# Block attention feeding a gated MLP: a place of its own for the odd tile's probabilities, and attention work in other slots

## Chip, cores, metric

One core of one Trainium2 chip runs the kernel. The metric is the device time of one execution in microseconds (us), the median over several runs; the kernel before took 499.02 us (three runs, 496.99 to 500.42). The engines are named as in the profile: PE (TensorE matmul), PEld (its weight loads), DVE (VectorE), ACT (ScalarE), POOL (GpSimd), SP (SyncE, whose queue issues all DMAs here).

## The reference

`q`, `k`, `v` are (8 batches, 8 heads, 576 positions, 64). Attention is local: each block of 64 positions attends to itself alone. Its output, heads side by side, is `x` (8, 576, 512), the input of a gated MLP:

```python
scores = scale * np.matmul(q_c, k_c.transpose(0, 1, 2, 4, 3))      # blocks of 64 positions
attn = np.exp(scores - np.max(scores, axis=-1, keepdims=True))
attn = attn / (np.sum(attn, axis=-1, keepdims=True) + 1e-09)
x = np.matmul(attn, v_c)                                           # -> (B, S, 512)
h = gelu(x @ w_in)                                                 # 512 -> 1024
u, v = h[..., :512], h[..., 512:]
v_n = (v - mean(v)) / np.sqrt(var(v) + 1e-06) * g_ln
v_s = np.einsum('ts,bsd->btd', w_sg, v_n) + b_sg[None, :, None]
out = x + (u * v_s) @ w_out
```

## The kernel before

**Tiles.** The 8 x 576 positions are 36 tiles of 128 positions, two blocks of 64 each. Two batches hold 9 tiles: 0 to 3 belong to the even batch, tile 4 is half of each, 5 to 8 belong to the odd batch. Tiles 0 and 1, 2 and 3, 5 and 6, 7 and 8 go as pairs; tile 4 goes by itself (the single tile). Further on, tile 9 is tile 0 of the next two batches, tile 13 is their single tile.

**Attention of a tile** has three steps, in code and tables named by a letter and the tile. S (`att_scores`): 16 matmuls of 64x64 for each tile into PSUM, then the softmax: maximum, subtraction, sums and reciprocal on DVE, exponential on ACT, normalization on DVE or POOL. T (`att_transpose`): DVE transposes 32x32 blocks, ACT and DVE copy them into the buffer `ptT`. O (`att_out`): 16 matmuls of 64x64 for each tile with the values `av`, after which `keep` writes `xh` (rounded) and `xf` on ACT and `xl` (the remainder) on DVE. Tiles 0 to 4 of the first two batches go through `first_scores` and a transpose on PE; tile 2 of these has its softmax on ACT, 16 small instructions.

**Buffers.** Probabilities `pt` have one buffer (tag "pt", bufs=1) for pairs and single tiles alike, so a single tile's softmax starts to write when the pair ahead has been read by its T, and the pair behind waits for the single tile. `ptT` has one buffer too, with two places. `av` has two buffers, one for each tile: the loads of a tile's values wait until O of the tile two ahead has read.

**MLP of a batch.** Units follow each other: v (5 or 4 units of 12 matmuls with 512 columns), u0 to u4, s0 to s3 and o0 to o2 (groups of 12 or 28 matmuls with 288 columns; u and o use products of sums of blocks, `tx`, `ts`, `wx`). `ORDER` fixes them. The list `SLOTS` says after which unit of a batch a step S, T or O of the tiles ahead is recorded: for odd batches key 1, for even ones key 0. The first two batches and the loading of the weights (W, w: v half of w_in; X, x: u half; Y: w_out) follow the list `START`. `REST_V` says for each quarter of the v half whether the low part is made by PE alone (p) or by DVE (v); with p, PE does one f32 matmul with `ident` more.

**What sets the order.** Nothing is issued as recorded. `Plan` collects every instruction, gives each a cost and a due time, and `run` fills the engines' queues; the result is a fixed order for each engine, DMAs included (all on SP's queue). `EARLY` shifts due times of named steps by thousands of ns. PE may take work from up to 10 us further down its list. Every instruction therefore carries one line number, L250, in the profile, and tiles' names tell them apart: `pm` is any PSUM tile, `qk` the queries and keys.

Of the kernel before, what the change touches and what calls it, by code (L numbers as in the profile page):

```python
# [12 lines left out]
F32 = mybir.dt.float32  # L13
# [11 lines left out]
B, H, S, D = 8, 8, 576, 64  # L25
P = 128
# [18 lines left out]


START = """
A0 L0 B0 A1 L1 L2 L3 B1 A2 A3 S0 W0 T0 S1 W1 S2 w0 w1 T1 W2 O0 O1 W3 w2 T2 S3 M0 w3 v00 O2 A4 T3 X0 O3 G0 S4 v01 A8 T4
O4 B8 x0 X1 v02 X2 x1 v03 X3 U1 v04 U0 x2 g0 g1 x3 g2 g3 P5 g4 F0 u02 u03 s00 T5 F1 T6 P7 s01 s02 Q5 T7 T8 s03 Q7 v10
v11 Y0 v12 v13 Y4 Y2 Y1 Y3 u10 u11 s10 u13 Y5 s11 Y6 Y7 u12 A10 s12 P9 B10 A12 o01 s13 T9 T10 o02 P11 A14 V0 V1 V2 V3  # L50
o03 o00 Q9 B12 T11 o10 o11 T12 B14 S13 A15 o12 Q11 o13 T13
"""

SUMS = {7: 0, 10: 1, 11: 2, 12: 3}
X_SUMS = {0: 0, 2: 1, 4: 2}

PE_TILES = 5

# [5 lines left out]

SLOTS = {1: "0:T0 3:S23 6:T2 8:T1 10:O01 12:S4 12:T3 14:O23 14:T4", 0: "0:O4 2:S56 5:T5 8:T6 9:S78 9:T7 10:O56 11:S9A 14:T8 14:O78"}


ON_POOL = ("a", "c", "n1", "n2", "n4", "t",)  # L70
# [10 lines left out]
G_BLOCK = {(0, 0): 0, (1, 0): 1, (1, 1): 2, (0, 1): 3}  # L81


REST_V, REST_U = "vppp", "pgvg"
ENGINES = ("tensor", "vector", "scalar", "gpsimd", "sync")
EARLY = {'X*': -8, 's03': 1, 'Y0': -2, 'P7': 3, 'v04': -4, 'X0': -1, 'w3': -1, 'W*': -1, 'g4': 5, 'Y7': -2}
AHEAD = 10000
SWITCH = 150
HORIZON = 25000
LATE, DMA_LATE = 60, 3000  # L90
WAIT = {"tensor": 100 + LATE, "gpsimd": 120 + LATE}
TABLES = {AF.Exp: 1, AF.Gelu_apprx_tanh: 2}
# [305 lines left out]
def block_attention_gated_mlp(ctx: ExitStack, tc: tile.TileContext, qkv, w_in, w_out, w_sg, g_ln, b_sg, out):  # L398
# [6 lines left out]
    att = pool("att", 2)  # L405
# [291 lines left out]
                nc.sync.dma_start(out=vts[t][j * D : (j + 1) * D, c * HP : (c + 1) * HP], in_=src)  # L697

    scale = 1.0 / math.sqrt(D)
    first_pts = att.tile([P, 3, H, D], F32, name="first_pts", tag="pt", bufs=1)  # L700
    first_ptT = att.tile([P, 2, HP, P], F32, name="first_ptT", tag="ptT", bufs=1)

    def att_scores(*tiles):

        if tiles[0] < PE_TILES:
            for t in tiles:
                first_scores(t)
            return
# [12 lines left out]
        nc.vector.tensor_reduce(by_slot, sc, axis=AX.X, op=ALU.max, negate=True)
        pt = att.tile([P, n, H, D], F32, name="pt", tag="pt", bufs=1)
        for i in range(n):
            nc.vector.tensor_tensor(
                pt[:, i].rearrange("p (c hp) s -> p c hp s", c=2), sc[:, :, i],
                by_slot[:, :, i].unsqueeze(3).broadcast_to([P, 2, HP, D]), op=ALU.add,
            )
        nc.scalar.activation(pt, pt, AF.Exp, scale=scale)
        den = nmax.rearrange("p (i h) -> p i h", i=n)
        nc.vector.tensor_reduce(den, pt, axis=AX.X, op=ALU.add)  # L730
        nc.vector.tensor_scalar(den, den, SM_EPS, None, op0=ALU.add)
        nc.vector.reciprocal(den, den)
        for i, t in enumerate(tiles):
            eng = pick("a") if t > last[1] else nc.vector
            eng.tensor_tensor(pt[:, i], pt[:, i], den[:, i].unsqueeze(2).broadcast_to([P, H, D]), op=ALU.mult)
            pts[t] = pt[:, i]

    def first_scores(t):

        qt = qks.pop(t)  # L740
        sc = ps_m.tile([P, 2, 512], F32, name="pm")[:, :, : HP * D].rearrange("p c (g s) -> p c g s", g=HP)
        for x in range(2):
            for e in range(2):
                for y in range(2):
                    for c in range(2):
                        h, j = 4 * x + 2 * y + e, (y + c) % 2
                        r, o = slice(c * D, (c + 1) * D), slice(j * D, (j + 1) * D)
                        nc.tensor.matmul(sc[o, c, 2 * x + e, :], qt[r, 0, h, :], qt[r, 1, h, :], start=True, stop=True)
        nd = small.tile([P, 2, H], F32, name="nmax", tag="nmax")
        nmax, den = nd[:, 0], nd[:, 1]  # L750
        by_slot = lambda a: a.rearrange("p (c hp) s -> p c hp s", c=2)
        nc.vector.tensor_reduce(nmax.rearrange("p (c hp) -> p c hp", c=2), sc, axis=AX.X, op=ALU.max, negate=True)
        pt = first_pts[:, t % 3]
        if t in ACT_SOFTMAX:
            nc.vector.tensor_scalar(nmax, nmax, scale, None, op0=ALU.mult)
            for h in range(H):
# [12 lines left out]
        pts[t] = pt

    ptTs = {}

    def att_transpose(t):
        pt = pts[t]
# [437 lines left out]
    for b in range(2, B):  # L1212
# [4 lines left out]
        for i, ((f, k), after) in enumerate(zip(units, slots)):  # L1217
# [61 lines left out]
```

## Time and profile before

| | |
|---|---|
| runs | 496.99, 499.02, 500.42 us; median 499.02 |
| profiled execution | 497.11 us, of which 495.3 us from its first to its last instruction (the span) |
| PE busy | 477.0 us (96%), 5076 matmul records |
| PE weight loads | 436.1 us |
| DVE, ACT, POOL busy | 421.4, 313.9, 127.4 us |
| granted TensorE clock | 0.999 of full speed over the span |
| ACT table loads | 34, 43.6 us |

Matmuls overlap in the records, so the pace of PE is read from the distance between the starts of two matmuls, not from the duration of one. An f32 matmul of the program stands as two records in the trace, the 64x64 ones too (1152 in the program, 2304 records).

### The profile page before, as it was taken

Reading aid. Unit: us, or ns where it says so; the run is one execution under the profiler, and the core shown is the slowest. Engines: PE = TensorE matmul, PEld = TensorE weight load, DVE = VectorE, ACT = ScalarE, POOL = GpSimd, SP = SyncE. Lnnn points to the kernel's source line nnn. Section 1 sums busy time; section 2 is a strip of 40 time slices with the busy share of each in tenths; the row PEclk is TensorE's granted clock in tenths of the full one; section 3 lists DMA queues with packets and bytes.
Section 4 is the critical chain, followed back from the end, with each engine's and each line's share of the span. In section 5 each row is a group of like instructions: output and inputs, shape, how many; then the busy total and the mean of one; then the engine's idle time right before and its main releaser. Section 6 shows DMA issues by size and latency. Waiting matters only on the chain.

```text
span 495.3 us, 12328 instructions
## 1 busy us (share of the span) xinstructions
PE 477.0 (96%) x5076; PEld 436.1 (88%) x5076; DVE 421.4 (85%) x771; ACT 313.9 (63%) x511; POOL 127.4 (26%) x115
## 2 busy tenths in 40 slices
PE   3999999999998999999999999999999999999996
PEld 2567898899997899888999899998999899998996
DVE  7978999997896899999879698988869698878466
ACT  4889598734365688646676587936675577834330
POOL 0104100200470668115301531115301341215000
PEclk9999999999999999999999999999999999999999
DMA  8965103123338504456153815436053823133112
GB/s 327 356 198 164 55 3 73 58 87 96 122 121 269 161 1 123 155 182 192 63 152 105 252 61 216 128 125 185 14 161 108 253 96 130 44 105 119 60 70 95
DMA packets 56140, 65.46 MB, mean 132 GB/s; under 512 B 35602, under 2 KB 45842, under 8 KB 56084
## 3 DMA queue, kind: packets, MB, share of 16 engines
q1 hardware_dynamic: 56084, 64.67, 40.8%
q8 instruction: 40, 0.66, 0.6%
q14 instruction: 16, 0.13, 0.1%
HBM read 52.07 MB, written 12.58 MB: 131 GB/s over the span
## 4 chain that ended last, share of the span: by engine, by line
PE 57%; DVE 26%; ACT 9%; DMA 5%; issue 2%; DVEq 0%; ACTq 0%; SPq 0%
PE pm L250 56%; DVE nmax L250 5%; DMA out_dram<-ot 3%; DVE ot L250 3%; DVE u L250 3%; DVE pt L250 2%; ACT ptT L250 2%; DVE gl L250 2%; DVE sm L250 2%; DVE ts L250 1%; DVE ptT L250 1%; ACT L250 1%; DVE xl L250 1%; DMA av<-qkv 1%; ACT z L250 1%
## 5 line engine op out<-in xcount | busy, mean ns | idle before, releaser
L250 PE MATMUL pm<-wsg,v 128*128 128x288 f32 x768 | 109.4, 297 | 0.0
L250 PEld LDWEIGHTS pm<-wsg,v 128*128 128x128 f32 x768 | 103.8, 188 | 0.9
L250 POOL TENSOR_TENSOR pt<-pt,nmax 128x512 f32<-128x512 f32 x27 | 31.0, 1164 | 162.9 <-DVE nmax L250 145.1
L250 PE MATMUL pm<-gh,wout 128*128 128x288 f32 x272 | 54.5, 299 | 0.8 <-DVE pt L250 0.8
L250 ACT ACT_TABLE_LOAD x34 | 43.6, 1283 | 18.4 <-DVE pt L250 9.3
L250 DVE TENSOR_TENSOR u<-pm,u 128x576 f32<-128x576 f32 x50 | 37.0, 750 | 19.2 <-PE pm L250 18.7
L250 PE MATMUL pm<-win_h,xl 128*128 128x512 f32 x128 | 51.8, 405 | 1.0 <-DVE xl L250 1.0
L250 ACT COPY ptT<-blocks 32x256 f32<-32x256 f32 (+1 forms) x93 | 44.2, 475 | 10.9 <-DVE blocks L250 9.1
L250 PE MATMUL pm<-win_l,xh 128*128 128x512 f32 x128 | 50.8, 397 | 0.0
L250 PE MATMUL pm<-win_h,xh 128*128 128x512 f32 x128 | 50.6, 395 | 0.0
L250 POOL TENSOR_TENSOR sm<-sm,neg_half 128x1 f32<-128x1 f32 x36 | 31.6, 878 | 69.5 <-DVE sm L250 41.5
L250 PEld LDWEIGHTS pm<-gh,wout 128*128 128x128 f32 x272 | 42.5, 188 | 1.8 <-DVE pt L250 1.1
L250 ACT CAST gh<-u 128x576 fp32r<-128x576 f32 x32 | 21.2, 672 | 27.2 <-DVE u L250 25.7
L250 DVE BATCH_NORM_STATS2 sm<-hs 128x6 f32<-128x512 f32 x36 | 24.8, 688 | 12.8 <-ACT hs L250 12.7
L250 PE MATMUL pm<-gl,wout 128*128 128x288 f32 x136 | 34.9, 295 | 0.0
L250 ACT ACTIVATE hs<-pm 128x512 f32<-128x512 f32 x36 | 21.3, 597 | 20.2 <-PE pm L250 13.2
L250 ACT ACTIVATE v<-hs,sm 128x512 fp32r<-128x512 f32 x32 | 23.1, 725 | 16.4 <-POOL sm L250 9.9
L250 PEld LDWEIGHTS pm<-win_h,xl 128*128 128x128 f32 x128 | 24.0, 188 | 7.8 <-DVE xl L250 2.3
L250 DVE TENSOR_TENSOR gl<-u,gh 128x576 fp32r<-128x576 f32 x32 | 25.2, 794 | 6.2 <-ACT gh L250 5.9
L250 PEld LDWEIGHTS pm<-win_h,xh 128*128 128x128 f32 x128 | 24.0, 188 | 5.7
L250 PE MATMUL pm<-xh,win_l 128*128 128x288 f32 x112 | 28.4, 300 | 0.0
L250 PEld LDWEIGHTS pm<-win_l,xh 128*128 128x128 f32 x128 | 24.1, 188 | 4.9
(151 smaller groups left out, 1155.7 us busy)
## 6 DMA issues: line engine op xcount, KB each, us to landing
qk<-qkv SPq DMA_DIRECT2D x31, 512.0 KB, 5.0
out_dram<-ot SPq DMA_DIRECT2D x31, 288.0 KB, 4.6
wx<-kept_u SPq DMA_DIRECT2D x10, 768.0 KB, 8.0
wx<-kept_o SPq DMA_DIRECT2D x10, 768.0 KB, 4.3
av<-qkv SPq DMA_DIRECT2D x116, 64.0 KB, 3.1
wsg<-w_in SPq DMA_DIRECT2D x4, 512.0 KB, 6.7
wout<-w_in SPq DMA_DIRECT2D x4, 512.0 KB, 4.8
st<-w_out SPq DMA_DIRECT2D x8, 256.0 KB, 2.8
```

Source lines behind the costliest of these rows:

```text
L250: getattr(getattr(self.nc, op.engine), op.method)(*op.args, **op.kwargs)
```

## The change

Single tiles get a buffer of their own for probabilities (tag "pt1"), and their transposed probabilities are written back into that buffer instead of `ptT`. In the first tiles the third place of `first_pts` becomes a tile of its own (`third_pt`). `START`, `SLOTS`, `SUMS`, `X_SUMS`, `EARLY` and `HORIZON` get other numbers, and the second quarter of the v half makes its low part on DVE (`REST_V`). The list `START` is long; one line stands for it.

```diff
-A0 L0 B0 A1 L1 L2 L3 B1 A2 A3 S0 W0 T0 S1 W1 S2 w0 w1 T1 W2 O0 O1 W3 w2 T2 S3 M0 w3 v00 O2 A4 T3 X0 O3 G0 S4 v01 A8 T4
+A0 L0 L1 L2 A1 B0 B1 A2 L3 A3 S0 W0 W1 T0 S1 S2 w0 w1 T1 W2 O0 O1 W3 w2 T2 S3 M0 w3 v00 O2 A4 T3 X0 O3 G0 S4 v01 A8 T4
...
-SUMS = {7: 0, 10: 1, 11: 2, 12: 3}
-X_SUMS = {0: 0, 2: 1, 4: 2}
+SUMS = {7: 0, 10: 1, 12: 2, 13: 3}
+X_SUMS = {0: 0, 1: 1, 5: 2}
...
-SLOTS = {1: "0:T0 3:S23 6:T2 8:T1 10:O01 12:S4 12:T3 14:O23 14:T4", 0: "0:O4 2:S56 5:T5 8:T6 9:S78 9:T7 10:O56 11:S9A 14:T8 14:O78"}
+SLOTS = {1: "2:T0 3:T1 6:S23 10:S4 10:O01 12:T2 13:T3 13:O23 14:T4 15:S56 15:O4", 0: "5:T5 8:T6 11:S78 11:O56 12:T7 14:T8 14:S9A 15:O78"}
...
-REST_V, REST_U = "vppp", "pgvg"
+REST_V, REST_U = "vvpp", "pgvg"
...
-EARLY = {'X*': -8, 's03': 1, 'Y0': -2, 'P7': 3, 'v04': -4, 'X0': -1, 'w3': -1, 'W*': -1, 'g4': 5, 'Y7': -2}
+EARLY = {'s03': 1, 'P7': 3, 'v04': -4, 'X0': -1, 'w3': -1, 'g4': 5, 'Y7': -2, 'x0': 8, 'W*': 12, 'X*': 3, 'Y0': -1}
...
-HORIZON = 25000
+HORIZON = 20000
...
-    first_pts = att.tile([P, 3, H, D], F32, name="first_pts", tag="pt", bufs=1)
+    first_pts = att.tile([P, 2, H, D], F32, name="first_pts", tag="pt", bufs=1)
+    third_pt = att.tile([P, 1, H, D], F32, name="third_pt", tag="pt1", bufs=1)
...
-        pt = att.tile([P, n, H, D], F32, name="pt", tag="pt", bufs=1)
+        pt = att.tile([P, n, H, D], F32, name="pt", tag="pt" if n == 2 else "pt1", bufs=1)
...
-        pt = first_pts[:, t % 3]
+        pt = first_pts[:, t % 3] if t % 3 < 2 else third_pt[:, 0]
...
-        if place == 0:
+        if place == 0 and t % 9 != 4:
             ptTs[0] = att.tile([P, 2, H, 2, D // 2], F32, name="ptT", tag="ptT", bufs=1)
...
-        ptT = ptTs[0][:, place]
+        ptT = pt.rearrange("p h (a s) -> p h a s", a=2) if t % 9 == 4 else ptTs[0][:, place]
```

Over the whole program PE has one matmul less (the f32 one with `ident` of the second quarter), DVE one instruction more (that quarter's low part), ACT 30 table loads instead of 34. The 1152 matmuls of 64x64 stand in 48 uninterrupted runs on PE before and in 37 after; up to the end of `START` there are 18 runs in both, behind it 30 before and 19 after.

On PE in batch 4, at the last u product (u4) and the s units around it (`tx`: sums of x; `wsg`, `v`: the s unit's operands; `qk` rows are S of tiles 25 and 26, `ptT` rows O of tiles 23 and 24), this stands before the change:

```order
L250 MATMUL pm_460<-tx_0_436,wx_0_439 128x288
L250 MATMUL pm_469<-qk_450 64x64 x16
L250 MATMUL pm_469<-qk_451 64x64 x16
L250 MATMUL pm_476<-wsg_0_160,v_431 128x288 x2
...
L250 MATMUL pm_476<-wsg_0_160,z1_0_86 128x288 x2
L250 MATMUL pm_477<-ptT_462,av_425 64x64 x16
L250 MATMUL pm_477<-ptT_462,av_435 64x64 x16
L250 MATMUL pm_460<-tx_0_436,win_l_83 128x288
```

The same place on PE after the change:

```order
L250 MATMUL pm_459<-tx_0_440,win_h_82 128x288
L250 MATMUL pm_473<-qk_430 64x64 x16
L250 MATMUL pm_473<-qk_431 64x64 x16
L250 MATMUL pm_478<-ptT_461,av_423 64x64 x16
L250 MATMUL pm_478<-ptT_461,av_434 64x64 x16
L250 MATMUL pm_481<-wsg_0_161,v_438 128x288 x2
```

An s unit stood between S and O; now O follows S without a wide matmul between them.

On PE at the end of `START`, around O of tile 13 (`pm_287` before, `pm_281` after, its values in `av`), where batch 2 begins with its first v unit (`pm_283` before, `pm_291` after), this stands before the change:

```order
L250 MATMUL pm_279<-gh_211,wout_0_194 128x288 x2
L250 MATMUL pm_283<-win_h_82,xl_258 128x512
...
L250 MATMUL pm_283<-win_h_82,xh_257 128x512
L250 MATMUL pm_287<-ptT_281,av_270 64x64 x16
L250 MATMUL pm_293<-win_h_82,xl_258 128x512
```

The same place on PE after the change (`pm_286` is S of tiles 14 and 15):

```order
L250 MATMUL pm_284<-gh_213,wout_0_191 128x288 x2
L250 MATMUL pm_286<-qk_242 64x64 x16
L250 MATMUL pm_291<-win_h_82,xl_259 128x512
...
L250 MATMUL pm_281<-pt_275,av_269 64x64
L250 MATMUL pm_286<-qk_276 64x64 x10
L250 MATMUL pm_281<-pt_275,av_269 64x64 x7
L250 MATMUL pm_286<-qk_276 64x64 x3
L250 MATMUL pm_281<-pt_275,av_269 64x64 x8
L250 MATMUL pm_286<-qk_276 64x64 x3
L250 MATMUL pm_291<-win_h_82,xh_258 128x512
```

O of tile 13 moved from behind the 12 matmuls of the v unit to behind five of them, and S of tile 14 moved ahead of the unit.

On DVE at the start, in the softmax of tile 1 (`nmax_106` before, `nmax_107` after; `wsg` and `wout` hold raw quarters of w_in there, in order wsg_0, wsg_1, wout_0, wout_1), this stands before the change:

```order
L250 TENSOR_TENSOR win_l_83<-wsg_0_94,win_h_82 128x512
L250 TENSOR_SCALAR wsg_1_97<-wsg_1_97 128x512
L250 TENSOR_REDUCE nmax_106<-pm_105 128x8
...
L250 TENSOR_TENSOR xl_115<-banks_90,xh_114 128x4x128
L250 TENSOR_SCALAR wout_0_98<-wout_0_98 128x512
```

The same place on DVE after the change:

```order
L250 TENSOR_TENSOR win_l_83<-wsg_0_95,win_h_82 128x512
L250 TENSOR_SCALAR wsg_1_96<-wsg_1_96 128x512
L250 TENSOR_REDUCE nmax_107<-pm_106 128x8
...
L250 TENSOR_TENSOR xl_116<-banks_90,xh_115 128x4x128
L250 TENSOR_REDUCE nmax_109<-pm_108 128x8
L250 TENSOR_TENSOR win_l_83<-wsg_1_96,win_h_82 128x512
```

The low part of the second quarter (the last row) is new on DVE, ahead of the work on the third and fourth quarter.

## Rows read from the trace of the kernel before

**Rows 1.** The page: the span, the busy time of each engine with its share of the span, and the chain of work that ended last, by engine.

```profile
span 495.3 us, 12328 instructions
...
PE 477.0 (96%) x5076; PEld 436.1 (88%) x5076; DVE 421.4 (85%) x771; ACT 313.9 (63%) x511; POOL 127.4 (26%) x115
...
PE 57%; DVE 26%; ACT 9%; DMA 5%; issue 2%; DVEq 0%; ACTq 0%; SPq 0%
```

**Rows 2.** Busy time by stretch, with its length, then PE, PEld, DVE, ACT and POOL busy us (number of instructions), granted clock, share of the DMA engines, GB/s.

```profile
128.00:160.00 32.00, 30.60 (x421) 28.70 (x423) 27.78 (x43) 17.35 (x29) 15.86 (x13) 1.00 0.55 175
200.00:220.00 20.00, 18.96 (x179) 17.14 (x178) 19.42 (x32) 12.67 (x19) 0.00 (x0) 1.00 0.43 157
...
372.00:440.00 68.00, 67.79 (x786) 63.29 (x787) 59.80 (x108) 46.80 (x71) 16.65 (x14) 1.00 0.37 114
```

**Rows 3.** The waits of PE over the whole span: who waited for whom, us in total, times, the longest.

```profile
PE pm L250 <- DMA qk<-qkv: 6.9, 2, 4.4
...
PE pm L250 <- DMA av<-qkv: 1.3, 1, 1.3
...
PE pm L250 <- DVE pt L250: 0.8, 1, 0.8
```

**Rows 4.** The timeline of PE around one run of 64 records of 64x64: start us, us, instruction, count. Matmuls of 288 columns are on both sides.

```profile
190.92 0.69 PE L250 MATMUL pm<-wsg,z 128*128 128x288 f32 x4
191.54 1.16 PE L250 MATMUL pm<-ptT,av 64*64 64x64 f32 x64
192.63 0.40 PE L250 MATMUL pm<-tx,win_l 128*128 128x288 f32 x1
192.87 0.43 PE L250 MATMUL pm<-tx,win_h 128*128 128x288 f32 x2
```

**Rows 5.** The timeline of PE around a run of 34 records in which two records of S (`qk`) stand among those of O; the first row is its first five, the last row the wide matmul behind it.

```profile
252.04 0.37 PE L250 MATMUL pm<-ptT,av 64*64 64x64 f32 x5
...
252.76 0.40 PE L250 MATMUL pm<-wsg,v 128*128 128x288 f32 x1
```

**Rows 6.** The timeline of DVE in the first 48 us: the low part of the first quarter of w_in, and `xl` of tile 1.

```profile
11.59 0.69 DVE L250 TENSOR_TENSOR win_l<-wsg,win_h 128x512 fp32r<-128x512 f32 x1
...
23.84 0.69 DVE L250 TENSOR_TENSOR xl<-banks,xh 128x512 fp32r<-128x512 f32 x1
```

**Rows 7.** The timeline of ACT in the first 48 us: the first of 16 softmax instructions of tile 2, and `xh` of tile 1 behind them.

```profile
20.86 0.31 ACT L250 ACTIVATE first_pts<-pm,nmax 128x64 f32<-128x64 f32 x1 [0.89 <-DVE nmax L250]
...
23.19 0.62 ACT L250 CAST xh<-banks 128x512 fp32r<-128x512 f32 x1
```

**Rows 8.** The timeline of PE in the first 45 us, in brackets the idle time ahead and what ended it: S of tile 1, an f32 matmul with `ident` (two records) and the next one, the first matmul of the first v unit.

```profile
8.03 1.13 PE L250 MATMUL pm<-qk 64*64 64x64 f32 x32 [2.53 <-DMA qk<-qkv]
...
19.15 1.02 PE L250 MATMUL pm<-wout,ident 128*128 128x512 f32 x2
20.07 0.38 PE L250 MATMUL pm<-wout,low 128*128 128x512 bf16 x1
...
25.02 0.40 PE L250 MATMUL pm<-win_h,xl 128*128 128x512 f32 x1
```

**Rows 9.** The timeline of PE and ACT around O of tiles 7 and 8, and the writing of their `xh`.

```profile
82.42 0.85 PE L250 MATMUL pm<-ptT,qkv_w 64*64 64x64 f32 x32
...
83.62 1.00 PE L250 MATMUL pm<-ptT,qkv_w 64*64 64x64 f32 x32 [0.35 <-issue]
...
84.85 1.01 ACT L250 CAST xh<-pm 128x1024 fp32r<-128x1024 f32 x1
```

**Rows 10.** The timeline of DVE behind it: `xl` of tiles 7 and 8.

```profile
86.81 1.29 DVE L250 TENSOR_TENSOR xl<-pm,xh 128x512 fp32r<-128x512 f32 x2 [0.25 <-ACT xf L250]
```

**Rows 11.** The timeline of PE at the end of `START`: O of tiles 11 and 12, the o unit behind it, the first and the last matmul of the first v unit of batch 2, O of tile 13.

```profile
150.61 1.18 PE L250 MATMUL pm<-ptT,av 64*64 64x64 f32 x64
151.72 0.53 PE L250 MATMUL pm<-gh,wout 128*128 128x288 f32 x2
...
155.01 0.40 PE L250 MATMUL pm<-win_h,xl 128*128 128x512 f32 x1
...
157.58 0.39 PE L250 MATMUL pm<-win_h,xh 128*128 128x512 f32 x1
159.25 0.95 PE L250 MATMUL pm<-ptT,av 64*64 64x64 f32 x15 [1.28 <-DMA av<-qkv]
```

**Rows 12.** The timeline of SP's queue there: start us, us that the issue took, DMA, count. The eight `av` transfers carry tiles 13 and 14.

```profile
152.09 1.16 SPq L250 DMA_DIRECT2D out_dram<-ot  x1
153.34 6.68 SPq L250 DMA_DIRECT2D av<-qkv  x8
```

**Rows 13.** The timeline of PE in batch 2, among the o units: an o product, half of an O, another product, and the wait behind it.

```profile
206.50 0.29 PE L250 MATMUL pm<-gh,wout 128*128 128x288 f32 x1
206.72 0.69 PE L250 MATMUL pm<-ptT,av 64*64 64x64 f32 x32
207.34 0.53 PE L250 MATMUL pm<-ts,wx 128*128 128x288 f32 x2
208.72 0.53 PE L250 MATMUL pm<-gh,wout 128*128 128x288 f32 x2 [0.84 <-DVE pt L250]
```

**Rows 14.** The timeline of DVE beside it: the subtraction of a pair's softmax, and a split of `ts`.

```profile
207.38 1.29 DVE L250 TENSOR_TENSOR pt<-pm,nmax 128x512 f32<-128x512 f32 x2
208.58 0.75 DVE L250 TENSOR_TENSOR ts<-u,ts 128x576 fp32r<-128x576 f32 x1
```

More of the change, by code (lines that the diff above doesn't have):

```diff
@@ L47 @@
 START = """
-A0 L0 B0 A1 L1 L2 L3 B1 A2 A3 S0 W0 T0 S1 W1 S2 w0 w1 T1 W2 O0 O1 W3 w2 T2 S3 M0 w3 v00 O2 A4 T3 X0 O3 G0 S4 v01 A8 T4
-O4 B8 x0 X1 v02 X2 x1 v03 X3 U1 v04 U0 x2 g0 g1 x3 g2 g3 P5 g4 F0 u02 u03 s00 T5 F1 T6 P7 s01 s02 Q5 T7 T8 s03 Q7 v10
-v11 Y0 v12 v13 Y4 Y2 Y1 Y3 u10 u11 s10 u13 Y5 s11 Y6 Y7 u12 A10 s12 P9 B10 A12 o01 s13 T9 T10 o02 P11 A14 V0 V1 V2 V3
-o03 o00 Q9 B12 T11 o10 o11 T12 B14 S13 A15 o12 Q11 o13 T13
-"""
-SUMS = {7: 0, 10: 1, 11: 2, 12: 3}
-X_SUMS = {0: 0, 2: 1, 4: 2}
+A0 L0 L1 L2 A1 B0 B1 A2 L3 A3 S0 W0 W1 T0 S1 S2 w0 w1 T1 W2 O0 O1 W3 w2 T2 S3 M0 w3 v00 O2 A4 T3 X0 O3 G0 S4 v01 A8 T4
+O4 x0 X1 v02 X2 x1 v03 B8 X3 U1 v04 U0 x2 g0 g1 g2 g3 P5 g4 x3 F0 u02 u03 s00 T5 F1 T6 P7 s01 s02 Q5 T7 T8 s03 v10 Y3
+Q7 v12 v11 Y0 Y4 v13 Y2 Y1 u10 Y5 u11 s10 u13 s11 Y6 Y7 u12 A10 s12 P9 B10 A12 o01 s13 T9 T10 o02 P11 A14 V0 V1 V2 V3
+o03 o00 Q9 o10 B12 T11 T12 B14 o11 S13 A15 o12 Q11 T13 O13 B15 o13 P14 A17
+"""
+SUMS = {7: 0, 10: 1, 12: 2, 13: 3}
+X_SUMS = {0: 0, 1: 1, 5: 2}
 PE_TILES = 5
```

## The prediction

> **What bounds the kernel now.** I read the page first. PE is busy for 477.0 of 495.3 us and DVE for 421.4, ACT for 313.9; the chain that ended last runs 57% on PE and 26% on DVE [rows 1]. So PE is the bound, with a DVE that in places has no room. The waits of PE say where it is not: 6.9 us for the first queries and keys, 1.3 us once for `av`, 0.8 us once for DVE, little else [rows 3]. The busy time by stretch shows the same three places: a start, 128 to 160 us (PE 30.60 of 32), 200 to 220 us (PE 18.96 of 20, DVE 19.42 of 20); in the long stretch 372 to 440 us PE has 67.79 of 68 [rows 2]. A change here can win in three ways only: less work on PE, a shorter start, or those few waits. None of the three is large: the waits named are 9.0 us together [rows 3], and 6.9 of that is the arrival of the first inputs.
>
> The profiled execution took 497.11 us, 1.9 us less than the median of the runs (499.02). I sum against the former and add 1.9 at the end.
>
> **The runs of 64x64 matmuls.** This is the main term. PE pays for going from wide matmuls to 64x64 ones and back. A run of 64 records takes from 191.54 to 192.63, 1.09 us, and its edges cost more than a matmul's 0.13: the last of the four rows ahead starts near 191.32, 0.22 before the run, and the first behind it has 0.24 to the next. That makes 1.09 + 0.09 + 0.11 = 1.29 us [rows 4]. A run of 32 takes from 206.72 to 207.34, 0.62, with an edge of 0.22 ahead [rows 13]; with the same edges 0.82. Two runs of 32 cost 1.64, one of 64 costs 1.29: a run has a fixed price of 0.35 us, and each record 0.0147. The change leaves 37 runs of 48, 11 fewer, all behind `START`: 11 x 0.35 = 3.9 us. But the joined runs put S beside O. The one such run of before alternates four times and takes 252.04 to 252.76, 0.72 for 34 records [rows 5], where a pure one would take 0.62 + 2 x 0.0147 = 0.65: 0.02 per alternation. The new order has 12 of them (7 joined runs, five in the run at tile 13): 0.2. I take **-3.7**. Were an alternation as dear as one edge (0.1), it would be -2.7; were it free, -3.9.
>
> The Trainium skill (TensorEngine Tiling (Array Packing), Key Properties) has a rule for this: a change of tiling mode drains TensorE, a change of tile within a mode does not. By it S beside O is free and the term would be -3.9. The trace agrees about the mode (0.35 us a run) and shows 0.02 per alternation where the rule has nothing.
>
> **The start.** Three things change up to the first v unit. The weights' quarters load ahead of tile 1's queries and keys, which were waited for until 8.03 [rows 8]: two transfers of 512 KB more ahead of them and one of 256 KB fewer. From S of tile 0 (4.4 us) to 8.03 three transfers of 1.25 MB together landed, 3.6 us, so 0.75 MB is an estimated 2.2 us later, 10.2. That S is short and PE was idle there anyway; DVE would take it up around 12.5 either way, so I cost it at 0.2. Second, DVE makes a second low part, 0.6 us by the distance to its neighbours (0.69 long, [rows 6]), for which PE loses one f32 `ident` matmul, 19.15 to 20.07, 0.92 us [rows 8]. PE is not the bound there, so the 0.92 is hidden under DVE, which is busy without a pause from 5.6 us to `xl` of tile 1 at 23.84 [rows 6]. Third, part of the fourth quarter's work on DVE now stands behind `xl` (about 1.1 us), and `xl` itself waits on ACT for the 16 softmax instructions of tile 2, 20.86 to 23.1, ahead of `xh` at 23.19 [rows 7]; these begin about 0.4 us later. The first v unit begins at 25.02 [rows 8]; I expect 25.3 to 25.5, its fourth quarter some 0.7 later than before, and half of that taken back in the gap that DVE had before S of tile 4. **+0.3**, between -0.9 (PE's matmul counts in full after all, the rest is hidden) and +1.5 (0.6 low part, 0.4 ACT, 0.5 the later quarter, nothing taken back).
>
> **O of tiles 7 and 8.** It ran in two halves, 82.42 and 83.62 [rows 9], because ACT was still copying `ptT`: the second half began 1.20 after the first, where 32 records take 32 x 0.0147 = 0.47; 0.7 us lost. Now a v unit stands ahead of it (155.01 to 157.58 and one step of 0.23, 2.8 us [rows 11]), which covers the wait. Late next is `xl` of tile 7: `xh` ends at 85.86 [rows 9], the first half of `xl` near 87.45 [rows 10], 2.95 us after that O, and the new order has 11 matmuls (2.6 us) before it is needed. 0.3 comes back as a wait. **-0.4**, between -0.7 and 0.
>
> **O of tile 13.** Its values can be loaded only when O of tiles 11 and 12 has read. That ended at 151.72, O of tile 13 began at 159.25: 7.5 us, of which the issue of the store ahead took 1.16 and the eight loads began at 153.34 [rows 11, 12]. PE had 3.3 us of an o unit and 2.8 of a v unit as cover and stood for 1.67 - 0.23 = 1.44 us [rows 11]. Now the cover is the o unit, S of tile 14 (0.8) and five matmuls (1.2): 5.3 us. The wait becomes 2.2: **+0.8**. Behind it in PE's order stand S of tile 15 and seven matmuls of the v unit, which wait too. Bounds: 0 (SP's queue has one store fewer at its end, the loads start 1.2 earlier) to +2 (DVE sets the stores' time, PE arrives earlier and waits more).
>
> **The o units of batch 2.** Between 207.34 and 208.72 PE waits for DVE, which did a pair's subtraction (1.29) ahead of the split of `ts` [rows 13, 14]: 1.38 - 0.27 = 1.1 us. The new order puts S of a tile pair and a whole product (1.6) before that product, so most of it is covered: **-0.9**, between -1.1 and 0.
>
> **New waits.** Softmax and transposes of the second pair move from the u units to the last s and the o units, where `gl`, `ts` and `ot` already fill DVE (97% in 200 to 220 us [rows 2]). The buffer of its own takes the single tile out of the pairs' way. The profile shows no row for what results; from below it is 0, from above one wait like the 1.1 us in three of five batches, +3.3. Near the lower end lies before's own record: DVE at 88% in 372 to 440 us cost PE 0.2 us [rows 2]. **+0.6**.
>
> Sum: -3.7 + 0.3 - 0.4 + 0.8 - 0.9 + 0.6 = -3.3. 497.1 - 3.3 = 493.8 for a profiled execution, 495.7 as a median. With all terms at their ends: -3.9 - 0.9 - 0.7 - 1.1 = -6.6 (a median of 492.4) and -2.7 + 1.5 + 2 + 3.3 = +4.1 (503.1; 2 for tile 13, 3.3 for new waits).
>
> **Rivals.** (a) More is won: S and O lie further from the DVE work that they wait for, and the small delays among the o units go as well; all terms near their good end, 492.4. For it: the fewer runs are certain, as an order. Against: behind 160 us little else is left to win [rows 2]. (b) DVE takes it back: PE is through with 3.7 us less and stands for DVE instead, since the same DVE work is due sooner. For it: 97% in 200 to 220 us, a chain with 26% DVE. Against: 12% of DVE is free in 372 to 440 us, 8 us, over twice what is won. Time: 498 to 500. (c) Slower: late O. O of the odd batch's second pair comes after o1 of the batch ahead, and the v units that need its `xl` follow 7 us behind by PE's own work. From `xh` to `xl` it took 85 to 88 us, 3.2 us [rows 9, 10]; if DVE is more than 4 us behind, v waits, in batches 3, 5 and 7, and the wait goes on into gelu and the s units. It decides from 3 us a batch: 3 x 3 = 9, less 3.3: 504.7. (d) `START` alone spoils it: +1.5 at the start, +2 at tile 13, nothing from tiles 7 and 8: 495.7 + 1.2 + 1.2 + 0.4 = 498.5, within the same bounds as (b).
>
> **How the numbers follow.** Forecast (493.7 to 497.7) 0.42, (a) 0.25, (b) and (d) 0.24, (c) 0.09. One per cent, about what a measurement of this kernel can tell from no change, is 5.0 us: 494.0 and 504.0 are the limits. Faster by more: all of (a) and a fifth of the forecast, 0.33. Slower by more: most of (c), 0.08. The rest 0.59. For 8 in 10 the range takes the forecast, (b) and (d) whole, and most of (a): 491.5 to 500.5. The forecast's own range is 493.7 to 497.7.
>
> **What would show it.** In the profile after: 37 runs of 64x64, joined ones of 128 records at 2.2 us; PE's first v unit near 25.4 us; O of tiles 7 and 8 in one piece; a wait of about 2 us for `av` of tile 13; no wait of 1 us for DVE near 205 us; PE's waits behind 220 us still under 1 us in sum. I am wrong if the runs cost the same joined (then S beside O is not free), if PE's waits for `xl` or `pt` behind 160 us come to more than 3 us, or if the start moves by more than 1.5 us.

## The result

The changed kernel takes 501.81 us (median of 18 runs, 498.42 to 503.47), the kernel before, beside it, 498.13 (18 runs, 496.23 to 500.42): ratio 1.0059, 95% interval 1.0039 to 1.0079. It is slower by more than the measurement's uncertainty and by less than one per cent. The forecast was 495.7 with a range up to 500.5, so the sign was wrong and the time lies outside the range.

| | before | after |
|---|---|---|
| profiled execution, us | 497.11 | 498.84 |
| median, us | 498.13 | 501.81 |
| median less profiled execution | 1.0 | 3.0 |
| PE idle in 128 to 200 us, of 72 | 1.40 | 4.01 |

Two things are to be explained: the profiled execution is 1.7 us slower where 3.3 less were expected, and the usual execution lies 3.0 us above the profiled one, where before it lay 1.0 above. The second can be followed, since each run comes with the mean granted clock of TensorE (as a share of its full speed). Of the 18 runs after, the three with 0.999 took 498.4 to 498.9, seven with 0.996 or 0.997 took 500.4 to 501.9, and eight with 0.990 to 0.993 took 502.2 to 503.5. The profiled one is among the first three.

### The profile page after: what moved, and what is told of

It is laid out like the page before. It is cut to its first block, busy times and chain, and to the rows that moved or that the text cites. A ratio compares the mean times of both kernels' runs of the same rounds, so it can differ in the third digit from the quotient of the medians.

```text
span 497.1 us, 12307 instructions
## 1 busy us (share of the span) xinstructions
PE 472.8 (95%) x5067; PEld 434.2 (87%) x5074; DVE 425.8 (86%) x772; ACT 309.7 (62%) x507; POOL 126.0 (25%) x115
## 4 chain that ended last, share of the span: by engine, by line
PE 64%; DVE 22%; DMA 4%; ACT 4%; issue 2%; POOL 2%; SPq 1%; DVEq 0%; ACTq 0%
PE pm L250 63%; DVE u L250 3%; DVE nmax L250 3%; DMA av<-qkv 2%; DVE ptT L250 2%; DVE ot L250 2%; DVE blocks L250 2%; DVE pt L250 2%; PE banks L250 1%; POOL r L250 1%; DVE xl L250 1%; DVE sm L250 1%; DVE v L250 1%; DMA out_dram<-ot 1%; DVE gl L250 1%
## 5 line engine op out<-in xcount | busy, mean ns | idle before, releaser
L250 PE MATMUL pm<-wsg,v 128*128 128x288 f32 x768 | 108.2, 296 | 0.1
L250 POOL TENSOR_TENSOR pt<-pt,nmax 128x512 f32<-128x512 f32 x27 | 29.7, 1116 | 155.2 <-DVE nmax L250 155.1
L250 ACT COPY ptT<-blocks 32x256 f32<-32x256 f32 (+1 forms) x84 | 40.0, 476 | 13.6 <-DVE blocks L250 11.6
L250 POOL TENSOR_TENSOR sm<-sm,neg_half 128x1 f32<-128x1 f32 x36 | 30.4, 847 | 65.9 <-DVE sm L250 61.9
L250 DVE SCALAR_TENSOR_TENSOR hs<-hs,sm,g_bc 128x512 f32<-128x512 f32 x36 | 30.2, 839 | 0.0
L250 POOL TENSOR_TENSOR xs<-xf 128x576 f32<-128x576 f32 x12 | 17.5, 1467 | 47.4 <-DMA out_dram<-ot 25.9
L250 DVE SCALAR_TENSOR_TENSOR v<-hs,sm,v 128x512 fp32r<-128x512 f32 x32 | 26.0, 815 | 3.8 <-ACT v L250 3.7
L250 PE MATMUL pm<-qk 64*64 64x64 f32 x992 | 21.1, 228 | 8.3 <-DMA qk<-qkv 8.3
```

Of the source, the lines that this page charges most:

```text
L250: getattr(getattr(self.nc, op.engine), op.method)(*op.args, **op.kwargs)
```

## The profile after

The page: span, busy time with its share and instructions, the chain that ended last [rows 1].

```profile
span 497.1 us, 12307 instructions
...
PE 472.8 (95%) x5067; PEld 434.2 (87%) x5074; DVE 425.8 (86%) x772; ACT 309.7 (62%) x507; POOL 126.0 (25%) x115
...
PE 64%; DVE 22%; DMA 4%; ACT 4%; issue 2%; POOL 2%; SPq 1%; DVEq 0%; ACTq 0%
```

PE works 4.2 us less and the span is 1.8 longer: PE stands (is idle) some 6 us more. Where, the busy time by stretch says (columns as in [rows 2]; behind each length PE's busy time). First before, in stretches that cover the whole body:

```profile
60.00:128.00 68.00, 67.63 (x686) 64.31 (x685) 61.67 (x136) 44.09 (x74) 5.25 (x6) 1.00 0.24 72
128.00:200.00 72.00, 70.60 (x913) 65.21 (x912) 63.44 (x105) 48.61 (x78) 42.75 (x34) 1.00 0.43 130
220.00:480.00 260.00, 259.50 (x2667) 241.97 (x2666) 213.86 (x377) 162.52 (x249) 69.15 (x60) 1.00 0.41 129
```

and after, with the stretch of 200 to 220 us that [rows 2] has for before:

```profile
60.00:128.00 68.00, 67.29 (x687) 63.76 (x686) 61.99 (x137) 43.89 (x74) 4.54 (x6) 1.00 0.23 71
128.00:200.00 72.00, 67.99 (x840) 63.11 (x839) 59.91 (x96) 44.84 (x74) 39.34 (x32) 1.00 0.39 120
200.00:220.00 20.00, 18.16 (x207) 16.45 (x205) 19.64 (x34) 9.94 (x16) 2.37 (x2) 1.00 0.54 176
220.00:480.00 260.00, 258.95 (x2699) 243.12 (x2699) 220.77 (x384) 164.83 (x252) 69.08 (x60) 1.00 0.41 130
```

The idle time of PE grows by 0.3, 2.6, 0.8 and 0.5 us; the other 1.7 lie in the first 60 us, where PE also works 1.7 us less. The large step is 128 to 200 us. The waits of PE in 60 to 500 us name it (columns as in [rows 3]):

```profile
PE pm L250 <- DMA av<-qkv: 2.1, 1, 2.1
PE pm L250 <- DVE z L250: 1.5, 1, 1.5
PE pm L250 <- DVE ts L250: 0.8, 1, 0.8
...
PE pm L250 <- DVE xl L250: 0.7, 1, 0.7
PE pm L250 <- ACT xh L250: 0.5, 1, 0.5
```

The first and the last of these are the place of O of tile 13 [rows 11]; in the timeline of PE:

```profile
157.05 0.40 PE L250 MATMUL pm<-win_l,xh 128*128 128x512 f32 x1
159.54 0.24 PE L250 MATMUL pm<-pt,av 64*64 64x64 f32 x1 [2.09 <-DMA av<-qkv]
...
161.34 0.27 PE L250 MATMUL pm<-pt,av 64*64 64x64 f32 x2 [0.46 <-ACT xh L250]
```

PE stands from 157.28 (a wide matmul is 0.23 from the next) to 159.54, and again for 0.46 within O (the releaser named is ACT, but the second half of the values is the likelier one, since `xh` isn't read by O; no run shows it). S of tile 15 stands in the same run and waits with it. The wait for `z` is DVE's order; in its timeline:

```profile
183.24 1.85 DVE L250 TENSOR_TENSOR tx<-xs,tx 128x576 fp32r<-128x576 f32 x1
185.02 0.70 DVE L250 STREAM_TRANSPOSE blocks<-pt 128x512 f32<-128x512 f32 x1
185.65 1.38 DVE L250 TENSOR_TENSOR u<-pm,u 128x576 f32<-128x576 f32 x2
187.05 0.74 DVE L250 SCALAR_TENSOR_TENSOR z<-hs,sm,z 64x512 fp32r<-64x512 f32 x1
```

`z`, which the s unit needs at 186.4, is written last, behind a split of `tx`, a transpose of the attention and two rows of `u`; PE goes on at 187.85.

## The experiments

Two theories were held against each other. Theory W: the loss is in the waits that the new orders make, each costing what it lasts. Theory C: TensorE's granted clock has a part in it. In the first four runs C puts this down to the new start. From the fifth run on it says: after PE has stood at tile 13, the clock falls to 1.2 GHz for several us in most executions, so that the stand is paid twice. Each run stands beside runs of the kernel before on the same chip, to which its ratio refers; the stands are those of the one profiled execution.

| run | stands at 150 to 165 us | median | ratio, 95% | runs at a mean clock of 0.998 or more |
|---|---|---|---|---|
| before, beside these | 1.3 | 498.5 to 499.2 | 1 | 25 of 75 |
| after | 2.1 + 0.5 | 501.81 | 1.0059 [1.0039, 1.0079] | 3 of 18 |
| e1_start_alone | 2.3 | 499.49 | 1.0016 [0.9997, 1.0035] | 1 of 12 |
| e2_rest_alone | 2.7 + 0.5 | 499.69 | 1.0028 [1.001, 1.0047] | 1 of 12 |
| e3_buffers_alone | 1.5 | 499.47 | 0.9998 [0.997, 1.0025] | 5 of 12 |
| e4_sums_back | 0.5 + 2.3 + 0.5 | 505.69 | 1.0146 [1.0115, 1.0177] | 0 of 6 |
| f1_o13_later | 0.7 + 2.5 | 499.37 | 1.0027 [0.9999, 1.0055] | 2 of 12 |
| f3_fill | 1.1, rest filled | 500.79 | 1.0063 [1.0036, 1.0089] | 7 of 12 |
| f6_before_later | none over 0.2 | 495.93 | 0.9942 [0.9919, 0.9965] | 9 of 9 |
| f7_before_filled | filled | 498.88 | 1.0011 [0.9991, 1.0032] | 12 of 12 |
| g1_later_all | none | 496.39 | 0.9950 [0.9924, 0.9976] | 7 of 9 |
| g2_later_old_start | none | 495.07 | 0.9921 [0.99, 0.9941] | 5 of 6 |

**Parts of the change.** START alone (on the kernel before, without its last attention steps, with its REST_V and its part of EARLY; of START's four lines the last is shown):

```
...
-o03 o00 Q9 B12 T11 o10 o11 T12 B14 S13 A15 o12 Q11 o13 T13
+o03 o00 Q9 o10 B12 T11 T12 B14 o11 S13 A15 o12 Q11 T13 o13
```

> The kernel before with the new START (without its last steps O13 B15 P14 A17), the new REST_V and the new EARLY of steps of START alone; buffers, SLOTS and the sums as before. Theory W (the time is lost in waits of PE that the new orders bring, at tile 13, before the s units and among the o units of batch 2): none of these is here, O of tiles 7 and 8 loses its 1.1 us and xl of tile 7 costs 0.9, the start +0.4, so -0.3 to +0.5 us against before, and the runs spread like those of before. Theory C (the start matters more than its 0.4 us, because PE works less in the first 15 us and the granted clock then comes out lower in most executions): +1 to +3 us in the median, with most runs at a mean clock of 0.990 to 0.997 instead of 0.999.

Everything but START (its last attention steps added to the old one; EARLY of START's steps goes back too):

```
...
-o03 o00 Q9 o10 B12 T11 T12 B14 o11 S13 A15 o12 Q11 T13 O13 B15 o13 P14 A17
+o03 o00 Q9 B12 T11 o10 o11 T12 B14 S13 A15 o12 Q11 o13 T13 O13 B15 P14 A17
...
-REST_V, REST_U = "vvpp", "pgvg"
+REST_V, REST_U = "vppp", "pgvg"
```

> The changed kernel with START (but for its last steps O13 B15 P14 A17, which the new SLOTS need), REST_V and the EARLY of START's steps as before. Theory W: the 11 runs saved (-3.9) and all the waits behind 150 us (tile 13 +1.4, before s0 of batch 2 +1.6, its o units +1.4, later 0.6), so +1 us in an execution at clock 0.999, about the whole loss of the change. Theory C: the executions run at 0.999 like those of before and the median is within 1.5 us of before.

The buffers alone (START, SLOTS, SUMS, EARLY, HORIZON of before):

> Only the buffers of the change: third_pt, tag pt1 and the transposition in place, with all tables as before. PE has 48 runs of 64x64 as before. Both theories: within 1 us of before. If the copy in place were slow in itself (ACT and DVE writing where the transposition had read), it would show here as +1 us or more.

The new attention slots with the old places of the sums:

```
-SUMS = {7: 0, 10: 1, 12: 2, 13: 3}
-X_SUMS = {0: 0, 1: 1, 5: 2}
+SUMS = {7: 0, 10: 1, 11: 2, 12: 3}
+X_SUMS = {0: 0, 2: 1, 4: 2}
...
-EARLY = {'s03': 1, 'P7': 3, 'v04': -4, 'X0': -1, 'w3': -1, 'g4': 5, 'Y7': -2, 'x0': 8, 'W*': 12, 'X*': 3, 'Y0': -1}
+EARLY = {'s03': 1, 'P7': 3, 'v04': -4, 'X0': -1, 'w3': -1, 'g4': 5, 'Y7': -2, 'x0': 8, 'W*': -1, 'X*': -8, 'Y0': -1}
```

> The changed kernel with EARLY of X* and W*, SUMS and X_SUMS as before. Theory W with the x sums and weight sums as the cause (they go ahead of the v chain on DVE in batch 2): the wait of 1.6 us before s0 of batch 2 and some 1 us of waits among its o units go, -2 to -3 us against the changed kernel. If the moved attention itself is the cause: no more than -0.5. Theory C: no difference in the clock against the changed kernel, median 500 to 502.

The buffers cost nothing that can be measured. START alone is within the uncertainty, the rest alone slower by 0.3%. The sums are not the loss: with their old places it is 0.8% worse than the change whole (505.69 to 501.81), so the new slots need their new places; neither theory had a time that high for e4. The first form of C fails: 11 of 12 runs of e2, which has the START of before, are at the lower clock too. What the four showed unasked is where the clock is lower. All four profiles have it at half behind tile 13; the stretches there, with columns as in [rows 2] (the clock is the third number from the end). e1:

```profile
160.00:162.00 2.00, 0.81 (x27) 0.73 (x30) 0.00 (x0) 1.12 (x1) 0.00 (x0) 1.00 0.28 65
162.10:165.40 3.30, 3.30 (x20) 2.55 (x10) 1.79 (x5) 1.85 (x6) 1.55 (x2) 0.50 0.75 238
```

e4, which waits for up to 2.1 us at a time for `ot` among the o units too:

```profile
162.50:169.20 6.70, 6.36 (x25) 5.09 (x26) 3.44 (x6) 3.47 (x7) 1.42 (x1) 0.50 0.88 257
217.10:220.40 3.30, 3.30 (x15) 3.25 (x15) 3.22 (x7) 0.73 (x2) 0.00 (x0) 0.50 0.64 207
```

0.50 is the level of 1.2 GHz, 1.00 that of 2.4 GHz. The Trainium skill (TensorE: Matmul & The Clock Gate, HAM oscillation) tells of a kernel that drops to the lower clock when TensorE waits for a DMA. The rows agree, though its waits are given as some 3 to 5 us, and those ahead of these stretches are 1.5 (e3) to 2.7 us (e2).

**The stand moved or filled.** O of tile 13 behind the second v unit of batch 2 (the first sums of x there follow it, since they read what it writes):

```
-o03 o00 Q9 o10 B12 T11 T12 B14 o11 S13 A15 o12 Q11 T13 O13 B15 o13 P14 A17
+o03 o00 Q9 o10 B12 T11 T12 B14 o11 S13 A15 o12 Q11 T13 o13 P14 A17
...
+            if (b, i) == (2, 1):
+                sooner(outputs, 13)
...
```

> The changed kernel with the outputs of tile 13 put behind the second v unit of batch 2, some 5.6 us later, so that its values are there (the first sums of x of batch 2 follow it, since they read what it writes). Theory C (the stand of TensorE before tile 13, 2.1 and 0.5 us in the profile after, also lets the granted clock fall to half for several us in most runs): no stand near 157 to 161 us, no run below a mean clock of 0.998, and the time is that of the runs after at 0.999, 498.7, less some 2.6 us of stands plus 0.35 us for one more run of 64x64: 496 to 497.5, ratio to before 0.994 to 0.998. Theory W (a stand costs what it lasts, the lower clock comes from elsewhere): 501.8 - 2.3 = 499.5, ratio 1.001, mean clocks of 0.990 to 0.997 as before.

It missed: the stand went from the values to the keys. In the timeline of PE:

```profile
157.89 0.50 PE L250 MATMUL pm<-win_h,xl 128*128 128x512 f32 x1
160.91 0.69 PE L250 MATMUL pm<-qk 64*64 64x64 f32 x32 [2.52 <-DMA qk<-qkv]
```

S of tile 15, put into START by the change, waits for its transfer just as long, and ten of twelve runs have the lower clock. But the profiled execution (clock 0.996) does not have it here: behind this stand of 2.5 us the clock is 1.00, and it is lower only in the start:

```profile
19.80:23.20 3.40, 3.40 (x34) 2.48 (x35) 3.25 (x8) 2.73 (x13) 0.00 (x0) 0.50 1.02 357
```

This kernel could not tell the theories apart, but it names a second early step, S of tiles 14 and 15, and a second place of the lower clock.

Extra matmuls in the stand, in the changed kernel (18) and in the one before (12, with `keep_clock(12)` behind the first v unit of batch 2). O of tile 13 of the former stands behind five matmuls of the v unit and is taken out of START:

```
...
+                if (b, m, i) == (2, 0, 5):
+                    keep_clock(18)
+                    sooner(outputs, 13)
...
-            nc.tensor.matmul(spare[:, 0, :P], ident, ident, start=True, stop=True)
+            nc.tensor.matmul(spare[:, 0, :P], ident, pts[13][:, 0:2].rearrange("p h a s -> p (h a s)"), start=True, stop=True)
...
```

> The changed kernel with 18 extra matmuls of 128x128 (their results are used by nothing) in front of the outputs of tile 13, which stand in its place behind five matmuls of the first v unit: TensorE works through the 2 us in which it stood, and the outputs of tile 13 start no earlier. Theory C: the stand is about as long in time but the clock stays up: mean clock 0.998 or more in all runs, 498.5 to 499.5, ratio about 1.000 to 1.002. Theory W: what was a stand is now work, nothing is won: 501.8 + 0.3 = 502.1, ratio 1.006 to 1.007, mean clocks of 0.990 to 0.997.

> The kernel before with 12 extra matmuls of 128x128 (their results are used by nothing) in the stand of 1.28 us ahead of the outputs of tile 13. Theory C: nothing is shorter, yet the runs of before that show a mean clock of 0.995 to 0.997 are gone: all at 0.998 or more, 496.5 to 497.5, ratio 0.997 to 0.999. Theory W: the times of before, ratio 1.000 to 1.001, with the spread of its clocks.

In the timelines of PE the filling is longer than planned, since each extra matmul is two records of 0.115 us (4.1 us for 18, 2.8 for 12). f3:

```profile
159.17 4.18 PE L250 MATMUL pm<-pt,ident 128*128 128x128 f32 x36
163.28 0.69 PE L250 MATMUL pm<-pt,av 64*64 64x64 f32 x32
```

f7:

```profile
157.93 2.84 PE L250 MATMUL pm<-ptT,ident 128*128 128x128 f32 x24
160.70 0.98 PE L250 MATMUL pm<-ptT,av 64*64 64x64 f32 x32
```

In f7, O of tile 13 starts 1.45 us later than before (160.70 to 159.25), the wide matmul behind it 1.1 us later (161.61 to 160.53). Under W the kernel would be that much slower, 499.6 to 500.0; under C it would be that much slower than the runs of before at 0.998 or more (median 497.2), 498.3 to 498.7. 498.88 was measured, nearer to C, but the interval of the ratio (0.9991 to 1.0032) holds both, and the ratio that C had on record (0.997 to 0.999) was missed. What decides is the clock: all 12 runs are at 0.998 or more, where 14 of 32 of before are beside them, with the same transfer and no stand. f3 agrees only in part: 7 of 12 runs keep the clock where 3 of 18 did, five don't (a stand of 1.1 us for `qk` is left), and its times, 1.3 above the upper bound of C, carry the filling's surplus.

The kernel before with its O of tile 13 one unit later (the first sums of x follow it, as in f1):

```
...
+            if (b, i) == (2, 0):
+                late, after = after, []
+            if (b, i) == (2, 1):
+                after = late + after
...
```

> The kernel before with the outputs of tile 13 behind the second v unit of batch 2 in place of the first, 2.8 us later, so that the stand of 1.28 us [rows 11] is covered. Theory C: the stand goes, and the lower clock that some runs of before show goes with it: all runs at a mean clock of 0.998 or more and within 0.8 us of each other, 495.5 to 496.5, ratio 0.995 or less. Theory W: only the 1.28 us go, the mean clocks spread from 0.995 to 1.000 as in the runs of before: ratio 0.9975.

As C says: no stand, all nine runs at 0.998 or more, 0.9942. The profiled execution gains 1.07 us (496.04 to 497.11), the median 2.6 (495.93 to 498.50): the stand and a bit more than as much again. One part of the expectation was missed: the nine runs lie 3.0 us apart (493.90 to 496.93), not within 0.8, so the clock is not the whole of the scatter.

**Both transfers covered.** The changed kernel with O of tile 13 behind the second v unit and S of tiles 14 and 15 behind the third (the first sums of x move as in f1); then the same with the old START:

```
-o03 o00 Q9 o10 B12 T11 T12 B14 o11 S13 A15 o12 Q11 T13 O13 B15 o13 P14 A17
+o03 o00 Q9 o10 B12 T11 T12 B14 o11 S13 A15 o12 Q11 T13 o13
...
+            if (b, i) == (2, 1):
+                sooner(outputs, 13)
+            if (b, i) == (2, 2):
+                sooner(scores, 14, 15)
...
```

> The changed kernel with the outputs of tile 13 behind the second v unit of batch 2 and the scores of tiles 14 and 15 behind its third, as the kernel before has the latter; all else as changed. (With the outputs alone moved, TensorE stood 2.5 us for the q and k of tile 15 in place of 2.1 us for the values of tile 13, and the clock still fell.) Theory C: with neither transfer waited for, no stand of over 1 us between 150 and 190 us and no granted clock at 1.2 GHz behind it: mean clocks of 0.998 or more in at least 10 of 12 runs, and 498.7 (after at 0.999) less 2.6 us of stands there and 1.5 us of the wait for z that came with them: 494.5 to 496.5, ratio 0.992 to 0.995. Theory W: the stands go but the mean clocks stay at 0.990 to 0.997: 501.8 - 4 = 497.8, ratio 0.998 to 0.999.

> The same with the START of before (its order of batches 0 and 1, with what belongs to it of EARLY and REST_V), new from batch 2 on: outputs of tile 13 behind the second v unit, scores of 14 and 15 behind the third. If the fewer runs of 64x64 behind 160 us are worth what their row says (-3.0 us of the -3.9 lie there) and START costs 0.4 us: 494 to 496, ratio 0.991 to 0.995, below the kernel before with only the outputs moved (495.9, 0.9942); clocks of 0.998 or more in at least 10 of 12 runs. If what the new places of batches 3 to 7 win is given back there: 496 or more, not below it.

g1 by stretch, the rows to hold against those of after above:

```profile
128.00:200.00 72.00, 71.47 (x870) 66.72 (x870) 64.88 (x102) 47.91 (x78) 39.36 (x32) 1.00 0.43 132
200.00:220.00 20.00, 18.06 (x228) 16.16 (x227) 19.47 (x34) 9.30 (x15) 2.95 (x3) 1.00 0.56 189
220.00:480.00 260.00, 258.38 (x2676) 242.81 (x2675) 222.57 (x381) 163.18 (x251) 70.70 (x60) 1.00 0.40 126
```

PE's idle time in 128 to 200 us falls from 4.01 to 0.53 us, and the profiled execution by the same 3.5 (498.84 to 495.36). `z` goes ahead of the split of `tx` on DVE (the timeline of DVE):

```profile
181.17 1.88 DVE L250 SCALAR_TENSOR_TENSOR z<-hs,sm,z 64x512 fp32r<-64x512 f32 x1
183.09 0.76 DVE L250 TENSOR_TENSOR u<-pm,u 128x576 f32<-128x576 f32 x1
183.76 0.75 DVE L250 TENSOR_TENSOR tx<-xs,tx 128x576 fp32r<-128x576 f32 x1
```

The ratio falls by 1.1%, 5.4 us. 3.5 of that are stands of the profiled execution; the other 1.9 go with the clock (7 of 9 runs at 0.998 or more, 3 of 18 in the changed kernel). In the other two stretches nothing is better than in the changed kernel, so what g1 won back was not lost there; the waits among the o units and behind them stayed. g2, with the old START, is 1.3 us below g1 and has the lowest median. Against f6, which has nothing of the change, its ratio is 0.2% less, with intervals that overlap. So most of what g1 and g2 gain on before is the stand that before had too, and little of the 3.9 us of the runs of 64x64 reaches the end. Where some of it goes the stretches behind 200 us show. f6:

```profile
200.00:220.00 20.00, 18.84 (x177) 16.92 (x176) 19.57 (x34) 11.81 (x16) 0.00 (x0) 1.00 0.45 157
220.00:480.00 260.00, 259.19 (x2666) 241.87 (x2665) 213.32 (x377) 162.09 (x249) 69.10 (x60) 1.00 0.40 127
```

g2:

```profile
200.00:220.00 20.00, 18.05 (x228) 16.16 (x227) 19.46 (x33) 9.30 (x15) 3.40 (x3) 1.00 0.57 185
220.00:480.00 260.00, 258.34 (x2675) 242.78 (x2674) 222.19 (x381) 162.57 (x251) 70.22 (x60) 1.00 0.40 126
```

PE's idle time there is 1.97 us in f6 and 3.61 in g2: 1.6 us more, with DVE busy for 222.2 of the 260 us behind 220 where it was for 213.3.

**Where the clock is lower.** The changed kernel profiled twice more:

> The changed kernel unedited, for a second profile: 15 of its 18 runs had a mean clock of 0.990 to 0.997, but the one profiled had 0.999, so its trace doesn't show where the clock is lower. Theory C: at 1.2 GHz from about 161 to 163 us on, behind the stands of 2.1 and 0.5 us, and where the mean is 0.993 or less also behind the wait for z at 186 us or those of 209 to 219 us; nothing behind 230 us. Theory W: stretches at 1.2 GHz lie elsewhere, or behind no stand.

> The same once more: theory C again expects the stretches at 1.2 GHz right behind the stands at 157 to 161, 186 and 209 to 219 us and none elsewhere behind 25 us; theory W expects them at other places than in the profile before this one.

h1 (502.52 us, mean clock 0.991) by stretch:

```profile
155.00:161.00 6.00, 3.34 (x66) 2.56 (x66) 2.71 (x6) 1.43 (x3) 0.00 (x0) 1.00 0.79 233
163.00:165.00 2.00, 1.99 (x15) 1.68 (x16) 0.43 (x2) 0.74 (x2) 0.00 (x0) 0.50 0.96 305
165.00:167.00 2.00, 2.00 (x7) 1.52 (x6) 1.97 (x3) 0.37 (x1) 1.96 (x2) 0.50 0.69 195
169.00:171.00 2.00, 2.00 (x10) 1.59 (x10) 1.77 (x5) 1.96 (x3) 0.17 (x1) 1.00 0.44 178
```

and h2 (500.44 us, 0.996), in the start:

```profile
16.00:20.00 4.00, 2.19 (x42) 1.54 (x37) 3.52 (x9) 3.33 (x7) 1.36 (x1) 1.00 0.97 362
20.00:24.00 4.00, 4.00 (x36) 2.53 (x36) 3.79 (x9) 3.33 (x18) 0.00 (x0) 0.57 1.02 352
24.00:28.00 4.00, 4.00 (x48) 2.58 (x46) 3.29 (x7) 2.78 (x8) 1.04 (x1) 1.00 0.79 263
```

h1 is as C expected at tile 13; behind the waits at 186 and 209 to 219 us, where C expected more of it for such a mean clock, it is not lower. h2 is not as expected: its clock was lower only at 20 us, behind a stretch of the start in which PE is busy for 2.19 of 4 us; f1, with the same START, shows it there too. So the profiles show two places and not one: tile 13 (e1 to e4, h1) and the new start (f1, h2). Nor is a stand enough by itself: behind 2.5 us in f1, 2.6 in h2 and 2.1 in the first profile of after, the clock stayed at 1.00, and so it did behind 1.2 us for `hs` at 236 us in f7 and 1.3 for `ptT` at 212 us in g1. That the old START goes with fewer such runs (g2, f6, f7: 26 of 27 at 0.998 or more, g1 with the new one 7 of 9) points the same way, but is too little to prove it.

## Why the prediction was wrong

Its terms against the profiled executions. The idle time in the records is too short a measure, since the records overlap; as in the prediction, a loss here is the distance between the starts of two matmuls less the usual one (0.13 us for 288 columns, 0.23 for 512).

| term | predicted | measured |
|---|---|---|
| runs of 64x64 | -3.7 | -3.7, stands left out: 30 runs behind `START` become 19, and joined ones of 96 and 128 records cost 1.8 to 1.9 and 2.2 to 2.3 us, as the prediction's prices say |
| start | +0.3 | +0.4 (last s unit of batch 0 68.42 to 68.83) |
| O of tiles 7 and 8 | -0.4 | -0.1: in one piece, 1.1 won there (0.7 was counted) and 1.0 lost at `xl` (0.3 was) |
| O of tile 13 | +0.8 | +1.4: 2.0 lost before (1.4 ahead, 0.6 within O), 3.4 after |
| o units of batch 2 | -0.9 | +1.3: 2.1 lost before, 3.4 after |
| new waits | +0.6 | +2.7: 1.7 for `z` at 186 us, 1.0 more than before behind 223 us |
| not in the sum | | -0.3: a delay of before between two halves of S at 195 us |
| sum | -3.3 | +1.7, and the execution +1.7 |

The waits among the o units of the changed kernel, in the timeline of PE (an O of 32 records takes 0.62 us where nothing is waited for [rows 13]; here it is 1.0 to the next product, and 0.3 more ahead):

```profile
211.38 0.29 PE L250 MATMUL pm<-ts,wx 128*128 128x288 f32 x1
212.52 1.73 PE L250 MATMUL pm<-ts,wx 128*128 128x288 f32 x11 [0.85 <-DVE ts L250]
...
215.56 0.29 PE L250 MATMUL pm<-gh,wx 128*128 128x288 f32 x1
216.09 0.85 PE L250 MATMUL pm<-ptT,av 64*64 64x64 f32 x32 [0.24 <-PE pm L250]
217.09 2.18 PE L250 MATMUL pm<-ts,wx 128*128 128x288 f32 x12
```

The main term held, and none of the prediction's signs of being wrong appeared (joined runs are cheaper, the waits for `xl` and `pt` behind 160 us are 0.8, the start moved by 0.4): they didn't watch the terms that failed. The start came out as summed, though not at the place: PE's first v unit begins at 25.13 us, not near 25.4, and DVE, said to be busy without a pause from 5.6 to 23.84 us, is so for 17.56 of these 18.24 us. Three steps failed in the profiled execution, and make up nearly all of the 5.0 us between -3.3 and +1.7.

**The new waits** (2.1 too low) were looked for behind 200 us, and bounded from below by the row of 372 to 440 us, where DVE has 12% free. The largest stands at 186 us, between the v and the s units of batch 2, and it went when S of tiles 14 and 15 and O of tile 13 stood later (g1).

**The o units of batch 2** (2.2 too low) were credited with the end of their wait, while the DVE that is late there (97% busy before, 98% after) was left as it was: the wait for `pt` went from there, and waits for `ts`, `ot` and `gl` took its place. That is rival (b). Its 498 to 500 were meant as a median, so 496.1 to 498.1 for a profiled execution; 498.84 and 501.81 lie above both, since tile 13 and the clock come on top. g2 has such waits too (1.3 for `ptT`, 0.4 for `ts`), without the stands of tile 13. That DVE's order is what makes them late is read from the profiles; no run changed that order alone.

**O of tile 13** (0.6 too low) had the length of its first wait sized rightly (2.2, measured 2.1), but not the second wait within O, which the kernel before has too: its 32 records take from 159.25 to 160.53, 1.28 us. And the price of the stand was taken as its length.

**From the profiled execution to the median** is the fourth step that failed: "add 1.9 at the end". That difference, from three runs, was taken for a constant of the kernel. In eighteen runs of before it is 1.0, and the change moved it to 3.0, with the share of runs that have a stretch at 1.2 GHz. h1, whose clock was at that level from about 161 to 168 us, takes 3.7 us more than the first profile of the same kernel (502.52 to 498.84; its first stand is 0.6 longer). In the runs at 0.998 or more the two kernels are 1.6 apart (498.84 to 497.2), as in the profiled executions; in the medians 3.7, by the ratio 2.9. The 1.3 to 2.1 between go with the clock. That PE's stand at tile 13 causes it is shown by f6 and f7 (21 of 21 runs without it, of which f7 has the same work and more) and borne out by g1; that the stand of the new start does so was only seen, in two profiles, not tried by an edit. Why one execution of the same kernel shows it and another doesn't, with the same stands in both (the first profile of after has them all at 1.00), stays open. So does why the wait for `av` is 1.3 us in before and 2.3 with START alone. The loads do not begin later there, but their issue takes longer: in SP's queue the eight of tiles 13 and 14 take 7.98 us from 153.49 in e1, 6.68 from 153.34 in before [rows 12]. But they take 7.72 in f6, which has the START of before, and the stand of the changed kernel is 2.1, 2.7 and 2.6 us in its three profiles: part of its length changes from execution to execution.

## What to carry to other kernels

A transfer that can only start when a buffer comes free needs its whole way as cover: count the matmuls between the last reader and the first user before a step is moved forward, and look at the next user in line too, since the stand goes there (`av`, then `qk`). A gain that is counted from fewer runs of 64x64 matmuls is real, but it is 0.35 us apiece, and one stand of 2 us eats six. Where the median lies above the profiled execution, ask for the clock of each run before taking the difference over to another kernel.

## What was not expected of the hardware

A stand of TensorE of 1.3 us at tile 13 (before) went with 50 of 75 runs at a lower mean clock, one of 2.1 to 2.7 us with 37 of 42 (after, e1, e2). With none over 0.2 us there (f6), or with useless matmuls in all of it (f7), there was none in 21; with none there but the other orders of the change, 3 of 15 (g1, g2). Runs of before at 0.998 or more have a median of 497.2 in each of three sets, those at 0.995 to 0.997 of 499.0 to 499.2: 1.9 us for a stand of 1.3. A filling that held PE up by another 1.1 us (f7) cost nothing that could be measured in the median (1.0011, 0.9991 to 1.0032).
